# The order of a prologue: two head pairs' scores ahead of the value pooling, and maxima in the exponential's bias

## The chip, the cores and the metric

The kernel runs on one core of a Trainium2 chip. The metric is the time on the device in microseconds; the median of three runs of the kernel before is 964.11 us.

## The reference

A pooled attention is followed by a feed-forward network with a squared ReLU. There are 8 batches, 8 heads, 576 tokens and a head dimension of 64; keys and values are averaged over 8 neighbouring tokens, so 72 keys stand against each query. The model width is 512, the hidden width 2048, the number of tokens in the network 8 x 576 = 4608. All is float32.

```python
k_p = k.reshape(B, H, Sp, pool, D).mean(axis=3)
v_p = v.reshape(B, H, Sp, pool, D).mean(axis=3)
scores = scale * np.matmul(q, k_p.transpose(0, 1, 3, 2))
scores = scores - np.max(scores, axis=-1, keepdims=True)
attn = np.exp(scores)
attn = attn / (np.sum(attn, axis=-1, keepdims=True) + 1e-09)
attn_out = np.matmul(attn, v_p)
x = attn_out.transpose(0, 2, 1, 3).reshape(B * S, H * D)
h = np.maximum(x @ w_in, 0.0)
out = (h * h @ w_out).astype(np.float32)
```

## The kernel before, in words

**Chunks and steps.** The 4608 tokens are worked on in 12 chunks of 384. For each chunk the hidden width is cut into 16 blocks of 128, which gives 12 x 16 steps. A step s issues, on TensorE (PE), the first product `hidden` of its block (tiles `h`) and the second product `project` of the block two steps before (tiles `o`); in between it issues the pieces of attention that were put down for it with `at(step, f, ...)`. Steps -5 to -1 issue only conversions of weights. From chunk 1 on each of these products is done as three products of rounded halves (`xh`, `xl`, `gh`, `gl`, and two words per weight); chunk 0 uses plain float32 products with the weights `wf` (for the first six blocks of `hidden`, and for all of `project`).

**Weights.** Each tile of weights is loaded (`raw_i`, `raw_o`), taken apart by two ACT instructions (`magnitude`) and put together again by three on DVE (`to_float32`, tiles `wf_i`, `wf_o`); later it is split into two words (`split_weights`). All of this happens during chunk 0, while the loads come in.

**Order.** Every instruction stays in program order on its engine. An engine that waits holds up everything behind it. The loads and stores are all issued from SP's queue.

**The front.** Before step -5 stands a prologue written out by hand: attention for chunk 0, which is four head pairs p = 0 to 3. `pool_k` sums groups of 8 keys on DVE and copies the result once more (tile `kp`); for batch 1 POOL does it. `transpose_k` (PE, tile `kps`) brings it to `kf`; the queries of a pair go through `transpose_q` (tile `qps`) to `st`. `token_scores` lays tokens on the partitions: 16 products into two PSUM banks (`sps`), then DVE's maxima (`tm`) and ACT's exponentials (`te`). `token_normalise` sums, inverts and multiplies on DVE. `token_turn` transposes the weights of attention (PE, tile `pps`) and copies them to `sc`. `pool_v_pair` sums batch 0's values with products against a matrix of ones (`vps`) and copies to `vp`; `pool_v` does it for batch 1 on POOL. `weigh_values` multiplies `vp` by `sc` (tile `av`) and copies to `x`, from which chunk 0's `hidden` reads. A function such as `token_scores` issues its PE work when called and returns `then`, which issues the rest.

The banks of chunk 0's scores are three that later hold `o`: pair p uses number (2p + j) mod 3 for j = 0, 1, so consecutive pairs share one. Tiles `kps`, `qps`, `vps`, `av` and those of `keep_busy` rotate through three other banks, `pps` through two.

`keep_busy(n)` issues n products of the identity with itself, whose result nobody reads; `IDLE` gives the two values of n (each product shows as two instructions in the profile).

**Chunk 1** has the same token layout, its pieces placed in chunk 0's steps by `EARLY`: pair p begins with `transpose_q` at step 16 + first[p], and the four pieces behind it follow one step each. Chunks 2 and on use another layout (`STEADY`).

**Even-odd order.** For chunk 0 the tokens of a tile are t = 4s + 2t' + two, for chunk 1 in each batch 2s + two. The copy to `sc` in `token_turn` puts them back in the order of the tokens while it copies.

Of the kernel before, what the change touches and what calls it, by code (L numbers as in the profile page):

```python
# [13 lines left out]
AF = mybir.ActivationFunctionType  # L14
ALU = mybir.AluOpType
# [22 lines left out]
def pooled_attn_relu2_ffn(  # L38
# [16 lines left out]
    PE, DVE, ACT, GP, SP = (InOrder(tc, e) for e in (nc.tensor, nc.vector, nc.scalar, nc.gpsimd, nc.sync))  # L55
    B, H, S, D = q.shape
# [3 lines left out]
    P = 128  # L60
    POOL = 8
    SP_ = S // POOL
    NPAIR = H // 2
    NFC = DFF // P
    NCC = DM // P
    CH = 384
    QT = 96
    NQ = CH // QT
# [5 lines left out]
    SCALE = 1.0 / (D ** 0.5) / POOL  # L74
    LAG, QL = 2, 4

    IDLE = (10, 2)
    STB, SCB, LD, OB = 1, 2, 4, 3


# [5 lines left out]

    STEADY = ((-22, -18, -14, -10), (0, 1, 3, 4, 5, 6, 7, 8))
    KV0 = -35
    EARLY = ((-16, -13, -10, -7), (0, 1, 2, 3, 4))

    KV_AT = ((0, 1, 4, 5, 8, 9), (2, 3, 6, 7, 10, 11), (7, 12), (12, 13, 16, 17, 20, 21, 24, 25))
    NKT = H * SP_ // QT
# [90 lines left out]
    def keep_busy(n):  # L183

        for i in range(0, n):
            if i % 8 == 0:
                t = ps_a.tile([P, 512], F32, name=f"idle_{n}_{i}", tag="a")
            PE.matmul(t[:, :P], lhsT=ident, rhs=ident, start=True, stop=True)
# [25 lines left out]
    def pool_k(b, i):  # L214
        if i % KT == 0:
            loaded["kp", b, i // KT] = sb.tile([QT, KT, 2, D], F32, name=f"kp_{b}_{i}", tag="kp", bufs=2)
        kp, kt = loaded["kp", b, i // KT][:, i % KT], loaded.pop(("k", b, i))
        if b == 1:
            by_halves(kp[:, 0, :], kt)
            GP.tensor_tensor(kp[:, 1, :], kt[:, :D], kt[:, D:2 * D], op=ALU.add)  # L220
        else:
            DVE.tensor_reduce(kp[:, 0, :], kt.rearrange("p (o d) -> p d o", d=D), axis=AX.X, op=ALU.add)
            DVE.tensor_copy(kp[:, 1, :], kp[:, 0, :])

    def new_batch(b):
        if b not in kv:
# [62 lines left out]
    def segments(c):  # L289
        t, segs = c * CH, []  # L290
        while t < (c + 1) * CH:
            b = t // S
            n = min((b + 1) * S, (c + 1) * CH) - t
            segs.append((b, t - c * CH, n))
            t += n
        return segs
# [101 lines left out]

    def token_banks(c, p, name, tag):
        if c:
            return [ps_a.tile([P, 512], F32, name=f"{name}_{c}_{p}_{j}", tag="a") for j in range(2)]
        if tag == "h":
            return [ps_h.tile([P, 512], F32, name=f"{name}_{c}_{p}_{j}", tag="h") for j in range(2)]
        return [ps_o.tile([P, 512], F32, name=f"{name}_{c}_{p}_{j}", tag=f"o{(2 * p + j) % NTT}") for j in range(2)]

    def token_scores(c, p):
        st = live.pop((c, p))
        ss = token_banks(c, p, "sps", "o")  # L410
        segs = segments(c)
        for t in range(NQ):
            h, b = 2 * p + t // 2, segs[t % 2 % len(segs)][0]
            for j in range(2):
                two = slice(j * D, (j + 1) * D)
                PE.matmul(ss[j][:QT, t * SP_:(t + 1) * SP_], lhsT=st[two, t * QT:(t + 1) * QT],
                          rhs=kf[b][two, h // KH, h % KH * SP_:(h % KH + 1) * SP_], start=True, stop=True)
        views = [x[:QT, :NQ * SP_].rearrange("p (t n) -> p t n", t=NQ) for x in ss]

        def then():  # L420
            m = sb.tile([QT, 4, 2, NQ], F32, name=f"tm_{c}_{p}", tag="tm", bufs=2)
            e = w_tile(F32, f"te_{c}_{p}")[:QT, :, :NQ * SP_].rearrange("p i (t n) -> p i t n", t=NQ)
            e = [e[:, i] for i in range(2)]
            for i in range(2):
                DVE.tensor_reduce(m[:, 0, i], views[i], axis=AX.X, op=ALU.max)
                if c:
                    DVE.tensor_scalar(m[:, 1, i], m[:, 0, i], -SCALE, None, op0=ALU.mult)
                else:
                    DVE.tensor_tensor(e[i], views[i], m[:, 0, i].unsqueeze(2).to_broadcast([QT, NQ, SP_]), op=ALU.subtract)
            for i in range(2):  # L430
                if c == 0:
                    ACT.activation(e[i], e[i], AF.Exp, scale=SCALE)
                for t in range(NQ if c else 0):
                    ACT.activation(e[i][:, t], views[i][:, t], AF.Exp, bias=m[:, 1, i, t:t + 1], scale=SCALE)
            live[c, p] = (e, m)

        return then
# [10 lines left out]
    def token_turn(c, p):  # L448
        e, _ = live.pop((c, p))
        pt = token_banks(c, p, "pps", "h")  # L450
        for i in range(2):
            for t in range(NQ):
                PE.transpose(pt[i][:SP_, t * QT:(t + 1) * QT], e[t // 2][:, i * 2 + t % 2], ident[:QT, :QT])

        def then():
            sc = sb.tile([SP_, 2, CH], F32, name=f"sc_{c}_{p}", tag="sc", bufs=SCB)
            order = "p (s t two) -> p two t s" if len(segments(c)) == 1 else "p (t s two) -> p two t s"
            for i in range(2):
                ACT.copy(sc[:, i].rearrange(order, t=NQ // 2, two=2),
                         pt[i][:SP_, :CH].rearrange("p (two t s) -> p two t s", t=NQ // 2, two=2))  # L460
            live[c, p] = (sc, None)

        return then
# [8 lines left out]
    def weigh_values(c, p):  # L472

        if p == 0 and c == 0:
            x0.extend(w_tile(F32, f"x_{c}_{i}")[:, :, :CH] for i in range(2))
        elif p == 0:
            xts[c] = (sb.tile([P, NPAIR, CH], F32R, name=f"xh_{c}", tag="xh", bufs=2),
                      sb.tile([P, NPAIR, CH], F32R, name=f"xl_{c}", tag="xl", bufs=2))
        sc, rb = live.pop((c, p))
        av = ps_a.tile([P, 512], F32, name=f"av_{c}_{p}", tag="a")  # L480
        for b, o, n in segments(c):
            for i in range(2):
                PE.matmul(av[i * D:(i + 1) * D, o:o + n], lhsT=kv[b][2][:, 2 * p + i, :], rhs=sc[:, i, o:o + n],
                                 start=True, stop=True)

        def then():
            if c == 0:
                ACT.copy(x0[p // 2][:, p % 2, :], av[:, :CH])
                return
            xh, xl = xts[c]  # L490
            if c == 1:
                split(xh[:, p, :], xl[:, p, :], av[:, :CH])
                return
            DVE.tensor_tensor(rb, av[:, :CH], rb, op=ALU.mult)
            split(xh[:, p, :], xl[:, p, :], rb)

        return then
# [41 lines left out]
    def project(c, fc):  # L539
        if fc == 0:  # L540
            accs[c] = [ps_o.tile([P, 512], F32, name=f"o_{c}_{t}", tag=f"o{t}") for t in range(NTT)]
        g, key = gts.pop((c, fc)), ("o", fc)
        for t in range(NTT):
            tt = slice(t * P, (t + 1) * P)
            if c == 0:
                prods = [(g[:, tt], wf[key])]
            else:
                prods = [(g[x][:, tt], wt[key][:, w, :]) for x, w in ((0, 0), (0, 1), (1, 0))]
            for i, (a, w) in enumerate(prods):
                PE.matmul(accs[c][t], lhsT=a, rhs=w, start=fc == 0 and i == 0, stop=fc == NFC - 1 and i == len(prods) - 1)  # L550

        def store():
            for t in range(NTT):
                ob = sb.tile([P, DM], F32, name=f"ob_{c}_{t}", tag="ob", bufs=OB)
                ACT.copy(ob, accs[c][t])
                dma(out[c * CH + t * P:c * CH + (t + 1) * P, :], ob)

        return store if fc == NFC - 1 else None

# [32 lines left out]
        land(key)  # L592
    issue_loads()
    keep_busy(IDLE[0])
    for i in range(KT + 2):
        pool_k(0, i)
    transpose_k(0, 0)()
    transpose_q(0, 0)()
    transpose_q(0, 1)()
    pool_k(0, KT + 2)  # L600
    keep_busy(IDLE[1])
    after = [token_scores(0, 0), transpose_k(0, 1)]
    for f in after:
        f()
    after = [pool_v_pair(0, 0), pool_v_pair(0, 1), token_scores(0, 1)]
    for f in reversed(after):
        f()
    after = [pool_v_pair(0, 2), pool_v_pair(0, 3)]
    transpose_q(0, 2)()
    transpose_q(0, 3)()  # L610
    for f in after:
        f()
    for i in range(NKT):
        pool_k(1, i)
    new_batch(1)
    for h in range(H):
        pool_v(1, h)
    for p in range(NPAIR):
        token_normalise(0, p)
        after = [token_scores(0, p + 2)] if p + 2 < NPAIR else []  # L620
        if p:
            weigh_values(0, p - 1)()
        keep_busy(IDLE[1])
        if p == 2:
            for key in first_keys:
                magnitude(key)
        token_turn(0, p)()
        for f in after:
            f()
    to_float32(*first_keys)  # L630
    weigh_values(0, NPAIR - 1)()
    for hf in range(2):
# [5 lines left out]
    t = 1e9  # L638
# [97 lines left out]
```

## Time and profile before

| | us |
|---|---|
| median of three runs | 964.11 (963.93 to 967.15) |
| the profiled execution | 964.33 |
| its span, first to last instruction | 962.6 |
| PE busy | 946.1 (98%) |
| DVE busy | 615.0 (64%) |
| ACT busy | 451.5 (47%) |
| POOL busy | 348.8 (36%) |

PE is TensorE's matmuls, PEld its weight loads, DVE is VectorE, ACT is ScalarE, POOL is GpSimd, SPq is the queue from which the transfers are issued. In a row of the timeline stand the start, the time from the start of the first to the end of the last of a group of instructions, the engine, the operation, the tile written and the tiles read, the shapes and the count; in brackets the idle time of the engine before it and what ended it. A row of the windows has the stretch, its length, then the busy time and the count of PE, PEld, DVE, ACT and POOL, then the granted clock of PE as a share of full speed, the busy share of the transfer engines and GB/s. A row of the chain has start, length and what the end of the kernel waited for in that time. Busy times of matmuls are modelled and may reach past the start of the next.

### The profile page before, as it was taken

How to read it: one execution, taken by the hardware profiler on the slowest of the kernel's cores; microseconds unless marked ns; L12 is line 12 of the kernel's file. 1: busy time of each engine (PE TensorE's matmuls, PEld its weight loads, DVE VectorE, ACT ScalarE, POOL GpSimd, SP SyncE). 2: the span in 40 equal slices, each digit the busy share in tenths (PEclk: the TensorE clock that was granted, in tenths of full speed). 3: DMA queues.
4: the chain of work that ended last, by engine and by line, in shares of the span. 5: the costliest groups of instructions: out<-in, count | busy, mean ns of one | idle time of the engine just before them, and what ended most of it. 6: DMA issues, size and time to landing. Idle time of an engine off the chain costs nothing.

```text
span 962.6 us, 13481 instructions
## 1 busy us (share of the span) xinstructions
PE 946.1 (98%) x4944; PEld 803.6 (83%) x4944; DVE 615.0 (64%) x1028; ACT 451.5 (47%) x909; POOL 348.8 (36%) x215
## 2 busy tenths in 40 slices
PE   7899999999999999999999999999999999999998
PEld 6456668888888888888888888888888888888997
DVE  7889886667865566677765656767776565453221
ACT  3789776754444344444344344434443434532322
POOL 3800144444444434344353444344443534440000
PEclk9799999999999999999999999999999999999999
DMA  9963112113112112112112112112211110100000
GB/s 256 319 237 116 61 33 78 35 50 98 52 31 77 32 34 67 48 52 82 52 44 77 30 35 79 38 30 69 82 50 39 68 32 18 58 10 9 33 1 34
DMA packets 51651, 63.65 MB, mean 66 GB/s; under 512 B 13936, under 2 KB 32192, under 8 KB 51584
## 3 DMA queue, kind: packets, MB, share of 16 engines
q1 hardware_dynamic: 51584, 62.78, 21.2%
q8 instruction: 39, 0.64, 0.3%
q14 instruction: 28, 0.23, 0.1%
HBM read 53.08 MB, written 9.68 MB: 65 GB/s over the span
## 4 chain that ended last, share of the span: by engine, by line
PE 88%; DVE 5%; DMA 4%; ACT 2%; issue 1%; SPq 0%; ACTq 0%; DVEq 0%
PE o L34 41%; PE h L34 39%; PE av L34 3%; PE sps L34 3%; DVE wf_o L34 2%; DVE wf_i L34 1%; PE qps L34 1%; DMA raw_o<-in_moe_w_out_dram 1%; DMA v<-in_v_dram 1%; DMA k<-in_k_dram 1%; ACT te L34 1%; DMA vv<-in_v_dram 1%; DMA raw_i<-in_moe_w_in_dram 1%; DVE tm L34 1%; DVE w_i L34 1%
## 5 line engine op out<-in xcount | busy, mean ns | idle before, releaser
L34 PE MATMUL h<-xh,w_i 128*128 128x384 f32 x1488 | 416.9, 341 | 0.0
L34 PE MATMUL o<-w_o,gh 128*128 128x512 f32 x1056 | 334.8, 398 | 0.0
L34 PEld LDWEIGHTS h<-xh,w_i 128*128 128x128 f32 x1488 | 272.8, 188 | 10.6 <-issue 1.4
L34 POOL PARTITION_ALL_REDUCE tot<-sc x80 | 201.4, 2564 | 210.1 <-issue 199.6
L34 PE MATMUL h<-xl,w_i 128*128 128x384 f32 x744 | 249.9, 336 | 0.0
L34 PEld LDWEIGHTS o<-w_o,gh 128*128 128x128 f32 x1056 | 192.4, 188 | 51.9 <-issue 16.5
L34 POOL PARTITION_ALL_REDUCE mx<-sc x80 | 117.8, 1519 | 287.1 <-ACT sc L34 287.1
L34 DVE TENSOR_TENSOR gl<-r,gh 128x384 fp32r<-128x384 f32 x176 | 143.5, 815 | 109.1 <-ACT gh L34 108.9
L34 PE MATMUL o<-w_o,gl 128*128 128x512 f32 x528 | 209.1, 396 | 0.0
L34 DVE TENSOR_TENSOR r<-r 128x384 f32<-128x384 f32 x160 | 105.6, 660 | 109.1 <-ACT r L34 108.8
L34 ACT CAST gh<-r 128x384 fp32r<-128x384 f32 x176 | 90.4, 514 | 150.3 <-DVE r L34 149.8
L34 PEld LDWEIGHTS h<-xl,w_i 128*128 128x128 f32 x744 | 139.7, 188 | 10.6 <-issue 2.9
L34 ACT ACTIVATE r<-h 128x384 f32<-128x384 f32 x192 | 94.2, 491 | 100.5 <-PE h L34 99.1
L34 PEld LDWEIGHTS o<-w_o,gl 128*128 128x128 f32 x528 | 99.1, 188 | 22.1
L34 DVE TENSOR_TENSOR st<-qps,st 64x384 fp32r<-64x384 f32 x80 | 60.8, 760 | 59.1 <-ACT st L34 58.3
L34 ACT CAST st<-qps 64x384 fp32r<-64x384 f32 x80 | 59.5, 744 | 56.9 <-PE qps L34 56.5
L34 ACT CAST xh<-rb 128x384 fp32r<-128x384 f32 x40 | 20.5, 513 | 94.6 <-DVE rb L34 94.6
L34 ACT ACTIVATE sc<-sc 72x384 f32<-72x384 f32 x80 | 39.7, 525 | 46.4 <-DVE sc L34 46.4
L34 DVE TENSOR_REDUCE vp<-v 72x64 f32<-72x512 f32 x48 | 51.0, 1062 | 0.0
L34 PE MATMUL av<-sc,vp 72*64 72x384 f32 (+1 forms) x256 | 45.6, 436 | 3.6 <-ACT sc L34 2.1
L34 PE MATMUL o<-wf_o,r 128*128 128x512 f32 x96 | 44.4, 598 | 0.0
L34 DVE TENSOR_REDUCE kp<-k 96x64 f32<-96x512 f32 x42 | 43.8, 1043 | 0.2 <-DMA k<-in_k_dram 0.2
(82 smaller groups left out, 702.1 us busy)
## 6 DMA issues: line engine op xcount, KB each, us to landing
k<-in_k_dram SPq DMA_DIRECT2D x48, 192.0 KB
out_dram<-ob SPq DMA_DIRECT2D x36, 256.0 KB
raw_i<-in_moe_w_in_dram SPq DMA_DIRECT2D x16, 512.0 KB
raw_o<-in_moe_w_out_dram SPq DMA_DIRECT2D x16, 512.0 KB
v<-in_v_dram SPq DMA_DIRECT2D x56, 144.0 KB
rb<-rd SPq DMA_DIRECT2D x80, 96.0 KB
q<-in_q_dram SPq DMA_DIRECT2D x30, 192.0 KB
q<-in_q_dram SPq DMA_DIRECT2D x32, 96.0 KB
```

The source lines that it names most:

```text
L34: return lambda *a, **k: self.tc.keep_in_program_order(f(*a, **k))
```

## The change

- The front has another order. After pair 0's scores come pair 1's, with the second half of the k pooling between them; `pool_v_pair` stands now one pair at a time in the loop over the pairs, beside the work of the same pair; `keep_busy` begins with 8 products instead of 10, and two of its five later calls, in the loop, are left out.
- Chunk 0's exponentials take the maxima as a bias for each token, as chunk 1 did: DVE scales the maxima, and ACT reads the scores from PSUM in four instructions for each bank. The subtraction on DVE goes.
- `sc`, and with it `x`, keep the even-odd order in chunks 0 and 1. `weigh_values` picks the columns of each batch for chunk 1, and the rows are put back where they are stored, six transfers for each of the two chunks instead of three.
- The second copy of the pooled keys moves from DVE to ACT, in the front and for batches 2 to 7.
- Chunk 1's pair 0 begins one step later (`EARLY`, -15 instead of -16).

```diff
-    IDLE = (10, 2)
+    IDLE = (8, 2)
...
-    EARLY = ((-16, -13, -10, -7), (0, 1, 2, 3, 4))
+    EARLY = ((-15, -13, -10, -7), (0, 1, 2, 3, 4))
...
-            DVE.tensor_copy(kp[:, 1, :], kp[:, 0, :])
+            ACT.copy(kp[:, 1, :], kp[:, 0, :])
...
                 DVE.tensor_reduce(m[:, 0, i], views[i], axis=AX.X, op=ALU.max)
-                if c:
-                    DVE.tensor_scalar(m[:, 1, i], m[:, 0, i], -SCALE, None, op0=ALU.mult)
-                else:
-                    DVE.tensor_tensor(e[i], views[i], m[:, 0, i].unsqueeze(2).to_broadcast([QT, NQ, SP_]), op=ALU.subtract)
+                DVE.tensor_scalar(m[:, 1, i], m[:, 0, i], -SCALE, None, op0=ALU.mult)
             for i in range(2):
-                if c == 0:
-                    ACT.activation(e[i], e[i], AF.Exp, scale=SCALE)
-                for t in range(NQ if c else 0):
+                for t in range(NQ):
                     ACT.activation(e[i][:, t], views[i][:, t], AF.Exp, bias=m[:, 1, i, t:t + 1], scale=SCALE)
...
-            order = "p (s t two) -> p two t s" if len(segments(c)) == 1 else "p (t s two) -> p two t s"
             for i in range(2):
-                ACT.copy(sc[:, i].rearrange(order, t=NQ // 2, two=2),
-                         pt[i][:SP_, :CH].rearrange("p (two t s) -> p two t s", t=NQ // 2, two=2))
+                ACT.copy(sc[:, i], pt[i][:SP_, :CH])
...
-        for b, o, n in segments(c):
+        segs = segments(c)
+        for t, (b, o, n) in enumerate(segs):
             for i in range(2):
-                PE.matmul(av[i * D:(i + 1) * D, o:o + n], lhsT=kv[b][2][:, 2 * p + i, :], rhs=sc[:, i, o:o + n],
-                                 start=True, stop=True)
+                x, y = av[i * D:(i + 1) * D, :CH], sc[:, i]
+                if c == 1:
+                    x, y = (a.rearrange("p (two t s) -> p t two s", two=2, t=2)[:, t] for a in (x, y))
+                elif c:
+                    x, y = x[:, o:o + n], y[:, o:o + n]
+                PE.matmul(x, lhsT=kv[b][2][:, 2 * p + i, :], rhs=y, start=True, stop=True)
...
-                dma(out[c * CH + t * P:c * CH + (t + 1) * P, :], ob)
+                rows = out[c * CH:(c + 1) * CH]
+                if c > 1:
+                    dma(rows[t * P:(t + 1) * P, :], ob)
+                    continue
+                rows = rows.rearrange("(s t two) d -> two t s d" if c == 0 else "(t s two) d -> two t s d", t=2, two=2)
+                for n in range(NQ):
+                    lo, hi = max(n * QT, t * P), min((n + 1) * QT, (t + 1) * P)
+                    if lo < hi:
+                        dma(rows[n // 2, n % 2, lo - n * QT:hi - n * QT, :], ob[lo - t * P:hi - t * P, :])
...
     keep_busy(IDLE[0])
-    for i in range(KT + 2):
+    for i in range(KT):
         pool_k(0, i)
     transpose_k(0, 0)()
     transpose_q(0, 0)()
+    keep_busy(IDLE[1])
+    pool_k(0, KT)
+    f = token_scores(0, 0)
     transpose_q(0, 1)()
+    f()
+    pool_k(0, KT + 1)
+    f = token_scores(0, 1)
     pool_k(0, KT + 2)
-    keep_busy(IDLE[1])
-    after = [token_scores(0, 0), transpose_k(0, 1)]
-    for f in after:
-        f()
-    after = [pool_v_pair(0, 0), pool_v_pair(0, 1), token_scores(0, 1)]
-    for f in reversed(after):
-        f()
-    after = [pool_v_pair(0, 2), pool_v_pair(0, 3)]
     transpose_q(0, 2)()
+    f()
+    transpose_k(0, 1)()
     transpose_q(0, 3)()
-    for f in after:
-        f()
...
     for p in range(NPAIR):
-        token_normalise(0, p)
-        after = [token_scores(0, p + 2)] if p + 2 < NPAIR else []
+        f = pool_v_pair(0, p)
+        if p + 2 < NPAIR:
+            g = token_scores(0, p + 2)
+            f()
+            token_normalise(0, p)
+            g()
+        else:
+            f()
+            token_normalise(0, p)
         if p:
             weigh_values(0, p - 1)()
-        keep_busy(IDLE[1])
+        if p > 1:
+            keep_busy(IDLE[1])
         if p == 2:
             for key in first_keys:
                 magnitude(key)
         token_turn(0, p)()
-        for f in after:
-            f()
```

## The prediction

> **What bounds the kernel now.** I read the page first, then the chain of work that ended last, then the busy times by window, then the timeline of the first 75 us.
>
> ```profile
> span 962.6 us, 13481 instructions
> ...
> PE 946.1 (98%) x4944; PEld 803.6 (83%) x4944; DVE 615.0 (64%) x1028; ACT 451.5 (47%) x909; POOL 348.8 (36%) x215
> ...
> PEclk9799999999999999999999999999999999999999
> ...
> PE 88%; DVE 5%; DMA 4%; ACT 2%; issue 1%; SPq 0%; ACTq 0%; DVEq 0%
> ```
>
> PE carries 88% of the chain, so the rest of the chain is about 115 us. The second slice of the clock row (24 to 48 us) shows that PE ran there at 0.7 of full speed. The merged chain says where PE takes over:
>
> ```profile
> 44.69 2.04 DVE wf_i L34 x3
> ...
> 113.54 0.46 DVE te L34
> ...
> 114.14 0.96 PE pps L34 x8
> ```
>
> From 114.14 us to the end the chain is PE's alone. From 44.69 to 113.5 us it runs over DVE and ACT (conversion of the weights, chunk 1's softmax), and before that over the front. So a change to the front pays only through the moment at which ACT and DVE can begin the conversions. These rows show that moment:
>
> ```profile
> 37.67 2.22 PE L34 MATMUL av<-sc,vp 72*64 72x384 f32 x4 [0.35 <-ACT sc L34]
> ...
> 39.83 4.47 PE L34 MATMUL h<-x,wf_i 128*128 128x384 f32 x8
> 39.93 0.48 ACT L34 COPY x<-av 128x384 f32<-128x384 f32 x1 [1.63 <-PE av L34]
> 40.31 0.67 ACT L34 ACTIVATE wf_o<-raw_o 128x512 f32<-128x512 f32 x1
> 41.01 0.65 DVE L34 TENSOR_SCALAR wf_o<-wf_o 128x512 f32<-128x512 f32 x1 [3.98 <-ACT wf_o L34]
> ```
>
> ACT waits 1.63 us for the last pair's av, copies it to x, and only then (program order) converts the next weights; DVE has idled 3.98 us for that. The copy of x ends at 40.41 us. This is the front's end, and all that follows hangs on it.
>
> **The front, walked through in both orders.** An instruction starts when its engine is free and its inputs are there, with about 0.07 us for a hand-over. The rows that give the durations and the old times:
>
> ```profile
> 3.38 4.34 PEld L34 LDWEIGHTS idle<-ident 128*128 128x128 f32 x20 [3.38 <-DVE ident L34]
> ...
> 3.52 1.02 DVE L34 TENSOR_REDUCE kp<-k 96x64 f32<-96x512 f32 x1 [0.20 <-DMA k<-in_k_dram]
> ...
> 4.57 0.19 DVE L34 COPY kp<-kp 96x64 f32<-96x64 f32 x1
> ...
> 9.36 0.52 PE L34 MATMUL qps<-ident,k 96*128 96x96 f32 x4 [0.23 <-DMA k<-in_q_dram]
> ...
> 10.29 0.90 PE L34 MATMUL sps<-kf,st 64*96 64x72 f32 x16
> ...
> 12.08 2.81 PE L34 MATMUL vps<-vv,ones 96*72 96x128 f32 x24 [0.49 <-DMA vv<-in_v_dram]
> ...
> 14.82 0.90 PE L34 MATMUL sps<-kf,st 64*96 64x72 f32 x16
> ...
> 17.47 0.80 DVE L34 TENSOR_REDUCE tm<-te 96x4 f32<-96x288 f32 x2
> ...
> 19.17 1.04 DVE L34 TENSOR_TENSOR te<-te,tm 96x288 f32<-96x288 f32 x2
> ...
> 23.05 1.56 ACT L34 COPY sc<-pps 72x384 f32<-72x384 f32 x2 [1.00 <-PE pps L34]
> ...
> 24.10 1.42 PE L34 MATMUL av<-sc,vp 72*64 72x384 f32 x4
> ```
>
> Three operations take a new form that chunk 1 already uses:
>
> ```profile
> 50.99 0.44 DVE L34 TENSOR_REDUCE tm<-sps 96x4 f32<-96x288 f32 x1
> 51.46 0.17 DVE L34 TENSOR_SCALAR tm<-tm 96x4 f32<-96x4 f32 x1
> ...
> 51.72 1.78 ACT L34 ACTIVATE te<-sps,tm 96x72 f32<-96x72 f32 x8 [1.48 <-DVE tm L34]
> ...
> 59.83 0.89 ACT L34 COPY sc<-pps 72x384 f32<-72x384 f32 x2
> ```
>
> So a pair's maxima cost DVE two reductions and two scalings, 1.2 us (2 x (0.44 + 0.17)); its exponentials cost ACT 1.78 us; its two sc copies, plain now, take 0.89 (chunk 1's layout is the nearest row) instead of 1.56.
>
> *To the first scores.* 16 weight loads instead of 20 end at 3.38 + 16 x 0.217 = 6.85. Three reductions from 3.52 end at 6.7, ACT's copy (nearest row 0.19) at 6.95. K's transposes to 7.5 and q's to 8.2 (the clock is still low: 0.5 and 0.7, against 0.52 for a set of q in the row at 9.36), st copied at 8.7 (0.48, the shape of x's copy), scores of pair 0 from 8.8 to 9.65. Old: 10.29, since pair 1's q, for which PE waited until 9.36, stood ahead.
>
> *Pair 1's scores.* Maxima 9.7 to 10.9, exponentials 10.5 to 12.3. One of pair 1's banks is the one that the first half of these reads, so its scores run from 11.5 to 12.4; old 14.82, behind 2.81 us of vps. DVE has two k reductions in between (to 13.0), then pair 1's maxima to 14.2 and pair 0's normalisation to 16.6 (2.4 us; the old rows give 19.17 + 1.04 - 17.47 = 2.7 beside POOL).
>
> *Pairs 2 and 3.* The second kf copy stands behind pair 1's exponentials on ACT (15.9); pair 2's scores 15.9 to 16.8, pair 0's turn to 17.5. ACT then has pair 2's exponentials first (17.5 to 19.3), so pair 0's sc ends at 20.1; old 24.6. Pair 1: scores of pair 3 to 19.7, av 19.8 to 21.1, turn 21.9, exponentials of pair 3 to 22.9, x, sc to 24.1. Pair 2: its vps fits in to 23.2, av 23.8 to 25.1, turn 26.3; ACT: x, four magnitude instructions at 0.57 (to 27.9; 0.67 alone in the row at 40.31, less the overlap), sc to 28.7. Pair 3: vps to 27.6, av 28.4 to 29.8, turn 30.9, sc 31.5, av 31.1 to 32.5, x at 33.0.
>
> The same walk over the old order gives 40.0 where the trace has 40.4, so I add 0.4: x at 33.4, **7.0 us sooner**. Some 4.5 of this stand at pair 0's sc, 1.3 are sc copies of pairs 2 and 3 (0.67 each), and about 1.5 is the clock (av at 2.22 instead of 1.42, the turns likewise). The first hidden matmuls, 4.47 us for 8 at the low clock, cost nothing either way: ACT's queue of conversions, not PE, holds the next step.
>
> **What is given back behind the front.** *POOL and DVE.* POOL pools batch 1's v until 46.8 us, started by its loads:
>
> ```profile
> 34.31 3.85 POOL L34 TENSOR_TENSOR v<-v 72x256 f32<-72x256 f32 x2
> ...
> 40.11 1.26 POOL L34 TENSOR_TENSOR v<-v 72x256 f32<-72x256 f32 x2
> ...
> 44.56 2.09 DVE L34 SCALAR_TENSOR_TENSOR wf_i<-wf_i,raw_i 128x512 uint32<-128x512 uint32 x2
> ...
> 46.18 0.66 POOL L34 TENSOR_TENSOR vp<-v 72x64 f32<-72x64 f32 x1
> ...
> 52.77 1.28 DVE L34 SCALAR_TENSOR_TENSOR wf_i<-wf_i,raw_i 128x512 uint32<-128x512 uint32 x2
> ```
>
> The same pair of instructions takes 2.09 us beside POOL and 1.28 without, so 0.8 lost. DVE works beside POOL from 41.0 to 46.8, and I put the whole loss at twice that pair's, an estimate of 1.7. Starting at 34, DVE works twice as long beside POOL. Between 0 (POOL gives way, as in its 3.85 us at 34.31 against 1.26 at 40.11) and 2.6 us more; I take **1.3**, the middle.
>
> *EARLY -15.* Chunk 1's pair 0 moves one step later, so its normalisation stands with split_x0 and its turn must wait for it on PE. Between -0.5 (the step's stall on ACT could shrink) and the whole normalisation, 2.4; I take **0.7**.
>
> *Loads.* The conversions would find their tiles landed only just:
>
> ```profile
> 29.34 1.24 SPq L34 DMA_DIRECT2D raw_o<-in_moe_w_out_dram x2
> ...
> 44.84 0.68 ACT L34 ACTIVATE wf_o<-raw_o 128x512 f32<-128x512 f32 x1
> ...
> 0.00:35.00 35.00, 26.81 (x207) 20.45 (x208) 27.82 (x67) 15.23 (x32) 18.66 (x41) 0.97 0.96 267
> ```
>
> Up to this pair of raw_o the loads add up to 9.4 MB (shapes of the code); 35 us at 267 GB/s are 9.3, and the second would be converted at 44.84 - 7.0 = 37.8. Price 0, with room for 1 us of landing time and little more.
>
> *At nothing:* the k copies on ACT in the steady loop (36 of about 0.2 us; ACT is 47% busy there, and what stands behind a copy, the step's Relu, is used two steps later); av of chunk 1 in another order, equally many columns; six more stores at 0.6 us of SP's queue each (1.24 for two, above), whose followers there are q loads four steps ahead of their use. If the k copies' cover were gone: 0.2 x 36 = 7 us.
>
> Sum: 7.0 - 1.3 - 0.7 = 5.0. The profiled execution took 964.33 us, so 959.3; it stands 0.2 above the median of 964.11, so **959.2 us**.
>
> **The clock, and the rule that speaks against this.** These windows, 3.4 us each:
>
> ```profile
> 9.00:12.40 3.40, 2.68 (x31) 2.23 (x31) 3.06 (x7) 1.16 (x3) 1.16 (x2) 1.00 1.11 248
> ...
> 15.80:19.20 3.40, 2.36 (x21) 2.12 (x21) 3.23 (x9) 1.20 (x4) 2.70 (x6) 1.00 1.09 265
> ...
> 29.50:32.90 3.40, 1.52 (x12) 0.87 (x11) 3.25 (x9) 3.40 (x7) 3.14 (x6) 1.00 1.00 292
> ...
> 39.70:43.10 3.40, 3.40 (x6) 1.85 (x6) 1.97 (x3) 3.17 (x6) 3.09 (x6) 0.50 1.05 388
> 43.10:46.50 3.40, 3.40 (x19) 2.33 (x18) 3.40 (x5) 3.40 (x8) 3.16 (x5) 1.00 1.07 298
> ```
>
> The clock halved behind a window with 1.52 us of PE and stayed full behind one with 2.36; it came back only behind the hidden matmuls. In the new order PE does 1.9 us in 9.0 to 12.4 (scores 0.65 and 0.85, q transposes 0.4), between the two, and 2.1 us or more in each later window. I take it as staying full, but this is the weakest place of the forecast. The Trainium skill, "TensorE: Matmul & The Clock Gate", Part 1 (the HAM clock gate), says that the gate looks at free-running windows of about 3.4 us and halves the clock behind an idle one; the trace agrees, with a low clock that lasted from 32.9 to 43.1 us, three such windows. The same page of the Trainium skill, Part 4 (PE-mode transpose), says that transposes do not count as busy in the same way; by that rule 9.0 to 12.4 us falls to 1.5 us, and the sum would be the first rival's. No row here separates transposes from the rest.
>
> **Rivals.** *The clock halves at 12.4 us and stays so until the hidden matmuls (slower).* From there the front's PE work (vps 4 x 1.4, av 4 x 1.42, sps 2 x 0.85, turns 4 x 0.8, rest 2) is 18 us; doubled and nearly without a gap it ends at about 48.5, and x is 8 us later than now. POOL is then done (1.7 back), the moved pair costs its 0.7: 964.3 + 8 - 1.7 + 0.7, about **971**; with the clock back one or two windows sooner, 965 to 969. It decides once x comes after 40.4, which is a low clock for over some 20 us. For it: the bare windows, the shorter warm-up (16 loads, not 20). Against: no window as empty as the one that tripped it.
>
> *The gain is lost again in DVE's queue* (POOL beside it at 2.6, the moved pair at 2.4, tiles 1 us late): 7.0 - 6.0, **963**. For it: the chain runs over DVE from 44.69 us on. Against: 0.8 of 2.09 is the worst that a pair shows.
>
> *Nothing is given back:* 7.0 to 7.5 net, **957**. For it: at 34.31 us POOL lost 2.6 us, and DVE need not.
>
> **How the numbers follow.** Forecast (gain 3 to 6.5): 0.52. Low clock: 0.23. Lost in DVE's queue: 0.13. Nothing given back: 0.12. What a measurement can tell from no change is 0.5%, 4.8 us, that is 959.3; the forecast lies at that line. Faster: 0.12 and 0.30 of the forecast's 0.52; same: its other 0.22 and the second rival; slower: the low clock. Range 956.0 (nothing given back, the moved pair's -0.5 and a little of the clock with it) to 969.0, which leaves out the long low clock; the likeliest case alone 957.8 to 961.3.
>
> **What would show it.** Right: scores of pair 1 near 11.5 us, no vps ahead of them; exponentials in groups of eight 96x72; the last x copy near 33.4; the granted clock at 1.00 throughout; DVE's conversions at about 34 to 47 us slower than later ones; the chain going over to PE near 109 us. Wrong: a clock of 0.50 between 12 and 30 us, x later than 36, or PE waiting for chunk 1's first turn by more than 2 us.

## The result: 0.6% slower, and the profile after

The changed kernel takes 971.45 us (median of 20 runs, 967.39 to 974.94) against 964.52 for the kernel before in the same session (20 runs): ratio 1.0064, 95% interval 1.0049 to 1.0080. The forecast was 959.2, range 956.0 to 969.0. The profiled execution took 969.88 us.

The page of the changed kernel, its lines on span, engines, clock and chain:

```profile
span 968.2 us, 13488 instructions
...
PE 947.6 (98%) x4932; PEld 805.7 (83%) x4932; DVE 613.3 (63%) x986; ACT 458.6 (47%) x975; POOL 347.8 (36%) x215
...
PEclk7999999999999999999999999999999999999999
...
PE 71%; DVE 14%; ACT 7%; DMA 5%; issue 3%; SPq 0%; DVEq 0%; ACTq 0%
```

PE does as much as before (947.6 us busy, 946.1 before), but only 71% of the chain is PE's instead of 88%: waits have come up all along the span, not in the front alone. The clock row has its low slice in the first 24 us now. (In the text below, the *lead* is how much earlier a group of `o` products starts than the same group in the kernel before, and the *gate* is whatever sets the granted clock.)

The busy times by window show that low clock (the columns are PE, PEld, DVE, ACT, POOL, granted clock, DMA share, GB/s):

```profile
8.80:12.20 3.40, 2.38 (x32) 1.81 (x33) 2.14 (x6) 1.85 (x9) 0.81 (x2) 1.00 1.10 248
12.20:15.60 3.40, 3.40 (x28) 3.27 (x25) 3.23 (x10) 2.55 (x13) 0.00 (x0) 0.52 1.09 254
15.60:19.00 3.40, 3.40 (x26) 2.95 (x26) 0.60 (x2) 1.33 (x5) 2.05 (x5) 0.50 1.08 271
19.00:22.40 3.40, 3.40 (x19) 3.40 (x20) 3.21 (x9) 2.35 (x10) 3.08 (x8) 0.50 1.08 316
22.40:25.80 3.40, 3.40 (x38) 2.53 (x37) 2.63 (x9) 1.77 (x9) 3.16 (x7) 0.97 0.99 365
```

The timeline gives what PE did ahead of the fall, and the front's end on ACT and PE:

```profile
9.06 0.90 PE L34 MATMUL sps<-kf,st 64*96 64x72 f32 x16
9.89 0.56 PE L34 MATMUL qps<-ident,k 96*128 96x96 f32 x4
11.02 0.39 PE L34 MATMUL sps<-kf,st 64*96 64x72 f32 x2 [0.57 <-DVE tm L34]
11.85 1.14 PE L34 MATMUL sps<-kf,st 64*96 64x72 f32 x14 [0.45 <-ACT te L34]
...
14.73 2.77 PE L34 MATMUL vps<-vv,ones 96*72 96x128 f32 x12
...
35.59 0.48 ACT L34 COPY x<-av 128x384 f32<-128x384 f32 x1 [0.95 <-PE av L34]
...
48.60 2.84 PE L34 MATMUL o<-wf_o,r 128*128 128x512 f32 x6
```

Pair 1's scores start at 11.02, as the new order wants (14.82 before). But they wait twice, and from 12.3 us each product takes double: 12 passes of vps take 2.77 us, where 24 took 2.81 before. The x copy ends at 36.07, 4.3 us sooner than 40.41, not 7.0. The first projection (the o group) starts 3.8 us sooner (48.60 against 52.42).

The waits of PE in the changed kernel (total, times, longest):

```profile
PE h L34 <- ACT r L34: 3.2, 1, 3.2
PE pps L34 <- DVE te L34: 3.0, 2, 2.3
PE kps L34 <- ACT kp L34: 2.1, 3, 0.7
PE sps L34 <- DVE st L34: 1.6, 4, 0.4
```

The first two have their long waits at 41.8 and 59.8 us. Behind the second the clock falls again, as the window and the third o group show (such a group takes 2.84 us at full clock):

```profile
63.20:66.60 3.40, 3.40 (x18) 2.27 (x19) 3.37 (x7) 0.55 (x2) 0.00 (x0) 0.55 0.66 201
...
64.83 3.88 PE L34 MATMUL o<-wf_o,r 128*128 128x512 f32 x6
```

Waits and low clock use up the lead: it is 5.7 us at the second o group, 2.0 at the third, and the fourth starts at 72.03 us, against 72.05 before. The other two kinds of wait are new and lie behind 114 us. There the trace falls behind that of before at seven places, by 0.5 to 0.9 us each (at 151, 247, 257, 475, 485, 704 and 713 us): an o group that was 0.22 us ahead at 114.72 us is 5.4 us late at 953.97.

So there are two losses to explain: 5.6 us in the steady loop, and a front whose gain is smaller and is then lost.

### The profile page after: what moved, and what is told of

Its sections match the earlier page's. It is cut to its first block, busy times and chain, and to the rows that moved or that the text cites. A ratio compares the mean times of both kernels' runs of the same rounds, so it can differ in the third digit from the quotient of the medians.

```text
span 968.2 us, 13488 instructions
## 1 busy us (share of the span) xinstructions
PE 947.6 (98%) x4932; PEld 805.7 (83%) x4932; DVE 613.3 (63%) x986; ACT 458.6 (47%) x975; POOL 347.8 (36%) x215
## 4 chain that ended last, share of the span: by engine, by line
PE 71%; DVE 14%; ACT 7%; DMA 5%; issue 3%; SPq 0%; DVEq 0%; ACTq 0%
PE o L34 33%; PE h L34 31%; PE av L34 3%; PE sps L34 2%; DVE kp L34 2%; DVE vp L34 2%; ACT gh L34 2%; DVE r L34 2%; DVE st L34 2%; DMA q<-in_q_dram 2%; ACT r L34 1%; DVE gl L34 1%; DVE wf_o L34 1%; PE qps L34 1%; DVE wf_i L34 1%
## 5 line engine op out<-in xcount | busy, mean ns | idle before, releaser
L34 POOL PARTITION_ALL_REDUCE mx<-sc x80 | 115.4, 1490 | 274.5 <-ACT sc L34 274.5
L34 DVE TENSOR_TENSOR r<-r 128x384 f32<-128x384 f32 x160 | 109.6, 685 | 126.8 <-ACT r L34 126.8
L34 PE MATMUL av<-sc,vp 72*64 72x384 f32 (+1 forms) x256 | 42.8, 425 | 2.6 <-ACT sc L34 1.3
L34 ACT COPY kp<-kp 96x64 f32<-96x64 f32 x42 | 10.3, 246 | 73.1 <-DVE kp L34 73.1
```

What stands on the lines that cost most here:

```text
L34: return lambda *a, **k: self.tc.keep_in_program_order(f(*a, **k))
```

## The experiments

Before has a median of 964.45, 964.64 and 963.83 us in the three sets of runs, so differences between sets are good to about 0.8 us. Each kernel below was run 6 to 12 times (the changed one 20 times); the ratio is not that of the two medians. The last column is the granted clock, averaged over the span, in the runs timed.

| kernel | median us | ratio to before, 95% | clock in its runs |
|---|---|---|---|
| changed | 971.45 | 1.0064 [1.0049, 1.0080] | 0.978 to 0.996 |
| e1: k copies on DVE | 967.44 | 1.0021 [1.0002, 1.0040] | 0.979 to 0.996 |
| e2: before, k copies on ACT | 971.37 | 1.0063 [1.0041, 1.0086] | 0.984 to 0.995 |
| e3: e1, pair 0 at -16 | 964.83 | 0.9993 [0.9978, 1.0008] | 0.982 to 0.993 |
| e4: e1, six idle products | 962.33 | 0.9970 [0.9951, 0.9988] | 0.993 to 0.996 |
| e5: e4, pair 0 at -16 | 965.74 | 0.9994 [0.9978, 1.0011] | 0.989 to 0.998 |
| e6: e5, half of v pooled by PE | **957.98** | **0.9920 [0.9899, 0.9941]** | 0.998 |
| e7: e1, 12 transposes | 962.64 | 0.9971 [0.9957, 0.9986] | 0.990 to 0.996 |
| e8: before, even-odd order kept | 963.57 | 0.9985 [0.9970, 0.9999] | 0.991 to 0.994 |
| e9: e6, pair 0 at -15 | 958.95 | 0.9952 [0.9936, 0.9969] | 0.996 to 0.999 |
| e10: e6, k copies on ACT | 963.37 | 1.0002 [0.9990, 1.0014] | 0.991 to 1.000 |
| e11: e6, three pairs of v on PE | 960.01 | 0.9957 [0.9937, 0.9976] | 0.989 to 1.000 |
| e12: before, half of v on PE | 964.80 | 1.0025 [1.0009, 1.0040] | 0.985 to 0.995 |

**The k copies (e1, e2, e10).** The first undoes them in the changed kernel for the steady loop, the other two put them on ACT in the kernel before and in the best one.

```
e1, on the changed kernel:
-            ACT.copy(kp[:, 1, :], kp[:, 0, :])
+            (DVE.tensor_copy if b else ACT.copy)(kp[:, 1, :], kp[:, 0, :])
e2, on the kernel before:
-            DVE.tensor_copy(kp[:, 1, :], kp[:, 0, :])
+            (ACT.copy if b else DVE.tensor_copy)(kp[:, 1, :], kp[:, 0, :])
e10, on e6: e1's line taken back
```

> The changed kernel with the second copy of the pooled keys back on DVE for batches 2 to 7; the front keeps it on ACT. Theory: in the steady loop ACT's copy waits for DVE's reduction of the keys, the step's Relu stands behind the copy, and DVE's square behind the Relu; PE pays for that at the six places where its start slips against the old kernel (near 247, 256, 475, 485, 704 and 713 us, 5.4 us in all). Then the median falls by 5 to 6 us, from 971.5 to about 966, PE no longer waits for ACT's kp copies, and the distance to the old kernel no longer grows behind 130 us. Rival: the slips come from the stores in pieces or from the even-odd order of chunks 0 and 1; then the time stays near 971.

> The kernel before with one edit: the second copy of the pooled keys on ACT for batches 2 to 7. Theory (ACT's copy in the steady loop costs 5.5 us by itself): 969.5 to 970.5, with PE waits of 0.7 us for ACT's kp copy. Rival (it costs only together with the changed front, or not at all): 964.5.

> The same best kernel (957.98 us) with the 36 k copies of the steady loop on ACT again. Theory (ACT's copy waits for DVE's reduction, the step's Relu stands behind it, the square behind that, and PE then waits for the copy or for st): PE's waits of 0.7 and 0.4 us for kp and st are back at the same six places and 5 to 6 us are lost: 963 to 964. Rival (the loss came with the later or low-clock front, and a faster front leaves ACT ahead): under 1 us: up to 959.

Measured, by the medians: 4.0 us less (e1, less than expected), 6.9 more (e2, more than expected), 5.4 more (e10, as expected; the cleanest, as the clock is nearly full in both kernels). The spread of the three comes with the clock, of which every set of runs caught another mixture. Among runs of equal mean clock the copies cost much the same everywhere: 5.5 to 6.0 us at 0.996 (the changed kernel 967.39 to 967.91, e1 961.94), 5.8 at 0.984 (medians of e2's three runs and of the five of before in the same set), 5.4 at 0.998 (e10 and e6). In e2 the trace loses 5.6 us against before, in e10 5.7 against e6, at the same seven places (the expectation's six leave out the first, of 0.5 us), and PE's waits over the steady loop of e10 are the two of the changed kernel to the tenth:

```profile
PE kps L34 <- ACT kp L34: 2.1, 3, 0.7
PE sps L34 <- DVE st L34: 1.6, 4, 0.4
```

e6 has no wait of PE there at all. The timeline of the changed kernel at one place shows the mechanism:

```profile
250.51 1.07 DVE L34 TENSOR_REDUCE kp<-k 96x64 f32<-96x512 f32 x1
251.61 0.24 ACT L34 COPY kp<-kp 96x64 f32<-96x64 f32 x1 [1.84 <-DVE kp L34]
251.76 0.48 ACT L34 ACTIVATE r<-h 128x384 f32<-128x384 f32 x1
252.28 0.56 DVE L34 TENSOR_TENSOR r<-r 128x384 f32<-128x384 f32 x1 [0.70 <-ACT r L34]
```

and the same step before:

```profile
247.46 0.49 ACT L34 ACTIVATE r<-h 128x384 f32<-128x384 f32 x1
...
248.32 1.07 DVE L34 TENSOR_REDUCE kp<-k 96x64 f32<-96x512 f32 x1
249.42 0.19 DVE L34 COPY kp<-kp 96x64 f32<-96x64 f32 x1
249.53 0.55 DVE L34 TENSOR_TENSOR r<-r 128x384 f32<-128x384 f32 x1
```

ACT's copy waits 1.84 us for DVE's reduction. The step's Relu stands behind it, ready long since, and DVE's square waits 0.70 us for that Relu; before, the Relu was done (247.46) ahead of that reduction, and the square followed the copy without a gap. So DVE, which was to save 0.19 us, loses 0.70, and its next reductions and differences reach PE late: 3 x 0.7 for kp and 4 x 0.4 for st, 3.7 us of waits. The other 1.9 us of the 5.6 stand at no wait that the profile names.

**The clock (e4, e7, e3).**

```
e4, on e1:
     transpose_q(0, 1)()
+    keep_busy(6)
     f()
e7, on e1: at that place 12 transposes of the 128x128 identity instead
e3, on e1:
-    EARLY = ((-15, -13, -10, -7), (0, 1, 2, 3, 4))
+    EARLY = ((-16, -13, -10, -7), (0, 1, 2, 3, 4))
```

> As e1, with six more idle products (12 instructions, about 1.3 us) where PE waits for the first exponentials, near 10.3 us. Theory: the granted clock halves at 12.2 us because the window from 8.8 to 12.2 us is too thin, and the length of that low clock is what spreads the runs over 7 us; then the clock is 1.00 from 9 to 30 us, the runs lie within 2 us of each other, and the median is 4 us or more below e1, near 961 to 962. Rival (the spread has another cause, or the idle products move the low clock to another window): median and spread as e1's.

> The kernel with the k copies on DVE and, in place of the six idle products (12 passes of 128 columns, 1.53 us) ahead of pair 1's scores, 12 transposes of the 128x128 identity. Theory (the gate takes transposes for work like any other): the clock stays at 1.00 until after 36 us, 962 to 963. Rival (the Trainium skill, TensorE: Matmul & The Clock Gate, Part 4: transposes do not count as busy in the same way): the granted clock falls to 0.50 near 12 us as without them, 965 to 968.

> As e1, and chunk 1's first pair one step earlier again, as in the kernel before. The prediction priced the move at 0.7 us of loss (between -0.5 and 2.4). In the profile of the changed kernel PE waits 2.3 us for that pair's normalisation and 3.2 us for the Relu. If the move costs: 0.7 to 2 us below e1, and no wait of PE for that turn. If the move helps: at or above e1.

Windows of e1 (PE, clock, DMA share, GB/s):

```profile
8.80:12.20 3.40, 1.88 (x30) 1.00 1.11 263
12.20:15.60 3.40, 3.36 (x32) 0.74 1.09 266
...
29.20:32.60 3.40, 3.40 (x15) 0.50 0.94 260
```

and of e7, whose first row is e4's too (there 3.40 us in 46 instructions, clock 1.00):

```profile
8.80:12.20 3.40, 3.40 (x38) 1.00 1.10 244
12.20:15.60 3.40, 3.35 (x39) 1.00 1.08 250
```

With the six products the clock is full until 41 us and the x copy ends at 32.64 us, 7.8 sooner than before; the time falls by 5.1 us. What they fill are PE's two waits ahead of pair 1's scores. The spread of e1 says the same: its one run at a mean clock of 0.996 took 961.94 us, like e4's 961.83 to 963.78 at 0.996, and those at 0.979 took 969.4. So the products take nothing off the work; they make the good case of the front the usual one. (e4's clock still falls twice later, at 41.4 and 62.0 us, for 3.4 us each, behind waits of PE of 3.4 and 2.0 us.)

e7 gives 962.64 and, in its profile, a full clock until 43 us: 12 transposes (1.48 us) do for the gate what 12 passes of products (1.53 us) do. The rule of the Trainium skill, "TensorE: Matmul & The Clock Gate", Part 4 (PE-mode transpose), that they don't count as busy in the same way, isn't borne out for these.

e3 shows the moved step where the clock is low in both kernels: back at -16 it saves 2.6 us by the medians, more than the 0.7 to 2 expected. That is not the price of the step by itself, as it changes with the clock: at mean clocks of 0.986 and 0.987 e3's runs take 962.1 to 964.0 us and e1's 966.35, but at 0.993 e3's take 964.8 to 965.3 and e1's only one 963.74.

**POOL (e5, e6, e9, e11, e12).** In e4 the lead is 7.2 us at the second o group (52.69), 2.1 at the fourth (69.92) and 2.3 at the eleventh (112.64). Ahead of that loss ACT stands still for 4.2 us, and PE for 2.0, in e4's timeline:

```profile
42.40 0.65 POOL L34 TENSOR_TENSOR vp<-v 72x64 f32<-72x64 f32 x1
43.02 2.03 POOL L34 TENSOR_TENSOR v<-v 72x256 f32<-72x256 f32 x2
...
43.11 0.67 ACT L34 ACTIVATE raw_o<-raw_o 128x512 uint32<-128x512 uint16 x1
...
43.52 2.07 DVE L34 SCALAR_TENSOR_TENSOR wf_o<-raw_o,wf_o 128x512 uint32<-128x512 uint32 x2
...
45.74 1.50 POOL L34 TENSOR_TENSOR v<-v 72x256 f32<-72x256 f32 x2
...
47.31 0.65 POOL L34 TENSOR_TENSOR vp<-v 72x64 f32<-72x64 f32 x1
...
47.99 0.69 ACT L34 ACTIVATE wf_i<-raw_i 128x512 f32<-128x512 f32 x1 [4.21 <-POOL vp L34]
...
60.00 1.06 PE L34 MATMUL pps<-ident,te 96*72 96x96 f32 x8 [1.97 <-DVE te L34]
...
62.28 4.32 PE L34 MATMUL o<-wf_o,r 128*128 128x512 f32 x6
```

The tile that the next weights are converted into seems to be one that POOL's last v pooling still reads, until 47.96 us. The profile doesn't show which tiles share a place, but it names POOL's last sum as what ended the wait, and the same happens in the changed kernel (ACT at 48.27, POOL's end at 48.23, a wait of 1.25 us) and in e7 (48.53 and 48.50). ACT's delay goes on over the split of chunk 0's x to DVE's normalisation of pair 0, for which PE waits, and behind this wait the clock falls: the third o group takes 4.32 us. POOL works without a gap from 15.6 us on, so it doesn't end sooner when the front does. The tests:

```
e5, on e4: EARLY's -15 back to -16
e6, on e5:
...
-    for h in range(H):
-        load_v(1, h)
+    for h in range(H // 2):
+        load_v(1, h)
+    for p in range(NPAIR // 2, NPAIR):
+        load_v_pair(1, p)
...
-    for h in range(H):
-        pool_v(1, h)
+    for h in range(H // 2):
+        pool_v(1, h)
...
+    for p in range(NPAIR // 2, NPAIR):
+        at(1, pool_v_pair, 1, p)
...
-    on_pe = (transpose_k,
+    on_pe = (pool_v_pair, transpose_k,
e9, on e6: -15 again
e11, on e6: pair 1 as well, in step 0
e12: e6's lines on the kernel before
```

> The kernel with the k copies back on DVE and six idle products ahead of pair 1's scores (962.33 us), and chunk 1's pair 0 back at step -16. Theory (what follows the front waits for POOL's last value pooling, which ended at 47.96 us and released ACT after 4.21 us of waiting, so that little hangs on the step before it): 961 to 962.3. Rival (the moved step is worth its 2.6 us whatever the clock does): 959.7.

> As the run before it, and heads 4 to 7 of batch 1's values are pooled by PE in step 1 with the matrix of ones (two groups like batch 0's, 1.5 us each, and two ACT copies) instead of by POOL. Theory (POOL's chain, 10.7 us of it for these heads, sets when the weights' tiles come free, and slows DVE beside it): POOL ends near 38 us, ACT's wait of 4.2 us for it is gone, DVE's pairs of conversions take 1.3 to 1.4 us instead of 2.08 from there on, PE's idle time before step 2 shrinks, and the lead of 5 to 7 us over the kernel before that is there at 50 us is kept at 112 us: 956 to 958.5. Rival (DVE's own work from 33 to 112 us is the bound, and POOL a bystander): within 1 us of the run before it.

> The kernel with k copies on DVE, six idle products and heads 4 to 7 pooled by PE (957.98 us), with chunk 1's pair 0 at step -15 instead of -16: what the moved step costs when neither the clock nor POOL is in the way. Theory (the step's normalisation stands with the split of chunk 0's x, and its turn makes PE wait, as the forecast had it): 0.7 more, up to 2.4: 958.7 to 960.4. Rival (the step costs nothing of its own): within 0.5 us of 957.98.

> The same best kernel with heads 2 and 3 of batch 1 pooled by PE as well, in step 0, so that POOL ends near 33 us. Theory (POOL beside DVE is all that is left to gain there): DVE's conversions from 33 to 38 us shrink from 1.67 and 2.08 to 1.28, about 1 us: 957. Rival (PE's 1.5 us more and ACT's copy in step 0 delay the step that ACT's queue hangs on): 958 to 959.

> The kernel before, with heads 4 to 7 of batch 1's values pooled by PE in step 1 and nothing else changed. Theory (in the kernel before, the front's end at 40.41 us and POOL's end at 46.8 are two bounds that nearly meet, so that taking away either alone gains little): 962 to 964. Rival (POOL is the bound by itself, and the front's order matters little): 959 to 960.

e5 missed both expectations: 3.4 us slower than e4. Its timeline has the pair's exponentials stuck, now ahead of the Relu that PE needs:

```profile
47.16 0.75 DVE L34 TENSOR_SCALAR wf_i<-wf_i 128x512 f32<-128x512 f32 x2
47.27 3.23 POOL L34 TENSOR_TENSOR vp<-v 72x64 f32<-72x64 f32 x1
47.84 1.28 DVE L34 SCALAR_TENSOR_TENSOR wf_i<-wf_i,raw_i 128x512 uint32<-128x512 uint32 x2
49.04 1.28 DVE L34 SCALAR_TENSOR_TENSOR wf_i<-raw_i,wf_i 128x512 uint32<-128x512 uint32 x2
...
50.53 1.77 ACT L34 ACTIVATE te<-sps,tm 96x72 f32<-96x72 f32 x8 [8.05 <-DMA raw_o<-in_moe_w_out_dram]
```

The profile names a DMA, but ACT starts 0.03 us behind POOL's last vp (47.27 + 3.23 = 50.50), and PE then has a gap of 6.1 us. That the wait is for POOL is read from these times. The earlier step, it seems, only brought another tile's wait for POOL ahead of more work. The wait is longer too: POOL's last sum takes 3.23 us, where it took 0.65 in e4, while DVE runs beside it at the times that it has without POOL. One of e5's twelve runs, with a mean clock of 0.998, took 959.88 us, which is the rival's number; so the stall seems not to come in every run.

e6 takes half of POOL's work away, and the stall is gone. Its timeline:

```profile
31.72 0.48 ACT L34 COPY x<-av 128x384 f32<-128x384 f32 x1 [0.95 <-PE av L34]
...
37.24 0.66 POOL L34 TENSOR_TENSOR vp<-v 72x64 f32<-72x64 f32 x1
...
39.57 0.75 DVE L34 TENSOR_SCALAR wf_o<-wf_o 128x512 f32<-128x512 f32 x2
40.24 1.28 DVE L34 SCALAR_TENSOR_TENSOR wf_o<-wf_o,raw_o 128x512 uint32<-128x512 uint32 x2
41.45 1.28 DVE L34 SCALAR_TENSOR_TENSOR wf_o<-raw_o,wf_o 128x512 uint32<-128x512 uint32 x2
...
45.44 0.69 ACT L34 ACTIVATE wf_o<-raw_o 128x512 f32<-128x512 f32 x1
```

POOL ends at 37.9, ACT goes on to the next weights at 45.44 right behind chunk 1's exponentials, DVE's set is at its free 0.75, 1.28 and 1.28, the clock is full from 5.4 to 73 us, and the lead of 7.9 us at the second o group (51.94) is still 7.4 at the eleventh (107.57). 957.98 us is the best of all, faster than both kernels by more than the intervals.

e9 prices the moved step with POOL out of the way: 1.0 us by the medians, within the 0.7 to 2.4 expected. The two kernels were run in different sets, which differ by 0.8 us in before, and three of e9's seven runs, at a mean clock of 0.996, take 960.6 to 960.8 us (the profiled one is among them and has a low clock from 96 to 103 us); the four at 0.998 or 0.999 take 957.7 to 959.0. So the step costs some 1 to 2 us, and not the same in every run. e9 also tells what POOL did in e4, which has the same -15: PE's wait for pair 0's turn is 0.37 us instead of 1.97, and the clock stays at 1.00 over the first four o groups.

e11 gains nothing and misses both expectations: POOL ends at 33.8, but PE waits 1.92 us for ACT in step 0 (qps for kf), and in the profiled execution, with 1.48 us of work at 36.0 to 39.4, the clock falls behind it; in its runs at 0.999 or 1.000 it takes 958.2 to 959.9, e6 957.3 to 958.5. e12 gains nothing (expected 962 to 964, got 964.8): with the old front ACT begins these conversions when x is done (at 44.82 us in the profiled execution, one of those with a long low clock; most of its runs, at 0.993 to 0.995, take 964.1 to 964.9), and POOL's early end is of no use. In the profile of before, ACT waits for POOL nowhere between 36 and 113 us. POOL is a bound only once the front is short. (e12 also puts 2.8 us of products more on PE, which no run prices by itself.)

**The even-odd order alone (e8).** Before, with the plain sc copies, chunk 1's av order and the stores in pieces.

> The kernel before, with only the kept even-odd order of chunks 0 and 1: plain sc copies, chunk 1's av in the other order of columns, and the stores of the two chunks in pieces. Theory (as the forecast priced it: nothing given back, sc copies of 0.89 instead of 1.56 us, two of them on the front's chain): the x copy ends 1 to 2 us before 40.41, and the time is 963 to 964.5. Rival (av in another order or the six more stores cost a microsecond or more where they stand): 965 or more, with a new wait for DMA or a slower av in the trace.

963.57, 1.1 us less than before, and the x copy ends at 38.64, 1.8 sooner, with sc copies of 0.85 for 1.56 us. No price for the stores or the av order shows.

## Why the prediction was wrong, step by step

**The k copies: the failed step.** The forecast put them at nothing, because "what stands behind a copy, the step's Relu, is used two steps later". PE uses it two steps later; DVE squares it right away, ahead of the next of the very reductions that PE waits for. The forecast followed the copy's follower to its last reader and not to its first, and did not ask what the copy itself waits for (1.84 us, against its 0.24). Price measured: 5.4 us, against 0. Its bound of 7 us held the size, by another sum: seven waits on PE, not 36 times 0.2.

**The clock: taken the wrong way, and said to be the weakest place.** It fell at 12.3 us as the first rival has it. What the forecast saw as two limits, 1.52 us of PE tripping the gate and 2.36 not, was none: the window ahead of the fall held 2.38 us. The rival's length failed too: low for 10.3 us in the changed kernel's profile, for some 20 in e1's, not until the hidden matmuls in the former. That the rival's 971 is the measured time is luck: it has a longer low clock, and nothing for the k copies. The price is the median's distance to the good case, 5.1 us from e1 to e4; with 5.4 for the k copies instead of the 4.0 of e1's mixture of clocks, 3.7 are left for it. The second fall, at 63.6 us, was not in the forecast.

**The front's walk: right.** Given a full clock, x ends at 32.64 (e4) where 33.4 was forecast; pair 1's scores and the groups of eight exponentials are there in the changed kernel.

**Loads at price 0: the wrong question.** It was asked when the weights land; they are in time. What is late is, as read above, the tile that they are converted into, held by POOL until 47.96 us. The forecast had POOL's end in its own rows, as DVE's hindrance only. Taking half of the pooling away is worth 3.4 us (e4 to e9; 2.8 if the 0.6 by which before differs in the two sets is taken off), the slower DVE included. In the changed kernel as it stands ACT's wait for POOL is only 1.25 us: this bound comes up as the others go.

**POOL beside DVE: mis-sized.** A set of three pairs of conversions takes 5.15 us in e4 (1.41, 1.67 and 2.07 at 40.60 to 45.52) and 3.31 in e6: 1.84 us lost. No single pair loses more than 0.8, as the forecast said, but all three pairs of a set lose, and for longer: over all sets from 33 us on DVE loses some 5.3 us in e4 and 2.0 in before (an estimate: the rows less the times that the same forms take without POOL). The forecast had 3.0 and 1.7. So 3.3 us more, where it took 1.3 and allowed 2.6.

**EARLY: right in size where POOL is out of the way.** 1.0 against 0.7, with the reservations above. PE's wait of 2.3 us for the first turn, named as a sign of error, appeared in the changed kernel and is 0.37 in e9.

**Even-odd order: right.** No run shows a cost.

**The sum.** The forecast's own terms give 959.1 (964.33 less 5.0 and 0.2), not 959.2; nothing hangs on it. From 971.45 the chain of kernels goes down by 4.0 (k copies), 5.1 (clock) and 3.4 (POOL) to e9's 958.95; this adds up by construction, and the shares hold only in this order. That 958.95 is also nearly the forecast is in part luck: e9 has idle products that the changed kernel lacks, and with half of the pooling gone the 1.3 us taken off for POOL has no place, so that the forecast for e9 would have been 957.9. What the runs do bear out is the term that the forecast counted, the front's gain: 7.0 forecast, and a lead of 7.4 us that lasts in e6. Each of three things that it had priced at nothing, or at too little, cost some 3 to 5 us.

## What to carry to other kernels

An engine that executes in order hands on its waits: before a small copy is moved to an idle engine, ask what the copy waits for and who first reads what stands behind it. A shorter front pays only as far as every tile it wants is free: list who holds the buffers, and until when. Where a new order leaves PE short gaps and the clock falls behind them, try a handful of idle products in the gaps: here six of them were worth 5.1 us. And compare runs of equal mean clock before a median is called a price.

## What the runs showed of the hardware

The same program ran at mean granted clocks of 0.978 to 0.996, with times from 974.9 to 967.4 us: whether, and for how long, the gate trips varies from run to run. That agrees with the free-running windows of about 3.4 us in the Trainium skill, "TensorE: Matmul & The Clock Gate", Part 1 (the HAM clock gate); the low stretch here, 12.3 to 22.6 us, is three of them, and each later one of 3.4 us (e4 at 41.4 and 62.0) is one. Not expected was that busy records don't lift the clock: e1 stayed at 0.50 through five windows in a row, 15.6 to 32.6 us, in which PE's records cover all 3.40 us. What the gate counts can't be read from those records, and no run here settles it.

POOL and DVE slow each other: DVE's set by 1.84 us in 3.31, POOL's last sum of a head from 0.32 to 0.65, and in e5 once to 3.23 while DVE ran at its free times. The Trainium skill, "Trainium Architecture — The Big Picture", "What this means for kernel authors", says that these two share a pair of ports under an exclusive lock; the runs agree that both lose.
